# Tail copies on GpSimd, two tiles that begin with main rows, a new slot plan, and W1 cast by columns in a fused attention and mixer kernel

## The chip, the cores and the metric

The kernel runs on one core of a Trainium2 chip. The metric is the device time in microseconds of one execution; a figure for a kernel is the median of several runs. The engines are TensorE (PE, matmuls and transposes), VectorE (DVE), ScalarE (ACT), GpSimd (POOL) and SyncE (SP, which here only issues DMAs).

## The reference

S = 2048 tokens, D = 576, F = 4608, fp32.

```python
xn = layernorm(x)
# A: sliding attention, 32 heads of 18, 8 keys at a distance of 2
qkv = xn @ wqkv                      # 576 x 1728
o = local_attention(q, k, v)         # each token sees itself and 7 earlier ones, 2 apart
A = o @ wo
# B: spatial shift mixer and MLP, on xn
h = gelu(layernorm(xn) @ w1)         # 576 x 576
hs = shift(h, +1, -1, +2, -2 by quarters of the columns) @ w2
x1 = xn + hs
B = x1 + gelu(layernorm(x1) @ w3) @ w4
out = x + A + B
```

## The kernel before

**Numbers.** fp32 operands are split into a high and a low part (hi is a rounded copy made by ScalarE, lo the difference made by VectorE), and each product is a handful of matmuls of such parts (`PAIRS`, `HALVES`). 576 = 4 × 128 + 64; the last rows of a contraction, the tails, are laid beside each other in one more block.

**Order.** Nothing is scheduled by a tool: every engine runs its instructions in the order in which the program names them, with waits where one engine needs another's tile. Plans (dictionaries from a unit's or slot's number to calls) say which side work is named behind which piece of TensorE's work.

**Prologue and plain units (0 to 90 us).** Y holds the sixteen 128-token tiles of x. `stats_x` and `norm_x` normalise a tile in place: VectorE makes the statistics, GpSimd the power −1/2 (L112), VectorE the product (L119). Every second `norm_x` also makes the factors `RS[1]` of the second layer norm, with VectorE's addition of 1e-5 (L220) between GpSimd's operations. `prep_x` turns a tile: `turned` first lets ScalarE copy the tails into a tile stg, four times beside each other (L286), then TensorE transposes four main blocks (L292) and two tail blocks (L294) into PSUM, and `cast_a` splits these into the operand xt. A unit `q_plain` is one token tile by one column group (288 columns) of wqkv: 14 matmuls (L363), a copy to stg and a DMA to the DRAM tensor qkvd. There are 36 units, and five stg tiles in all, which tail copies and results share.

**The p loop (90 to 208.7 us).** For the tiles 6 to 15 the product is done in Strassen-Winograd form: a pair of token tiles (p = 3 to 7) by three column groups, seven products of 7 matmuls each (`step`, L504), 21 slots for a p. PSUM has the banks ca, cb and cc, two each, and one bank pair pp, in which the next pair is turned: `low2` (the odd tile) and `up2` (the even one), each followed by sums that VectorE and ScalarE write to a region of Y (`raw_s`) and by casts to xt (`cast_upper`, `cast_s`). ScalarE and VectorE copy or add the products into keep tiles (L515, L531, L537), which SP spills to qkvd (L348).

**Turned tiles of the second norm.** `z_turn(t)` scales a tile by ScalarE (z, L467), and VectorE transposes it by 32 x 32 blocks into st (L128, L129), one buffer for four tiles. After every fourth, `put` writes st to DRAM as xd with four DMAs (L136). `get` loads xd again as the operand z of the mixer, and `split_x` casts it.

**W1 and Y.** W1 is loaded into Y[0:5] in the loop, so these tiles of Y are first copied to DRAM (`away`, ysp, L474), and loaded back after W1 is cast (`split_w1`, L495).

**The mixer (208.7 to 268 us)** goes over four blocks of 512 tokens; a block has four tiles of 14 matmuls by W1 (L638) and one of 9 by W1R, the remaining columns (L653). Its casts and loads are named between these tiles. The stages after that (W2, MLP with attention beside it) are not touched.

SP's queue is in order, and every DMA on it waits for the one issued eight before it.

Of the kernel before, what the change touches and what calls it, by code (L numbers as in the profile page):

```python
# [57 lines left out]
def fused_block(ctx, tc, x, wqkv, wo, w1, w2, w3, w4, out):  # L58
# [27 lines left out]
    mhalf = base.tile([128, 1], F32, name="mhalf")  # L86
    sgn = base.tile([128, 1], F32, name="sgn")
# [105 lines left out]
    XO = {"A11": 0, "A12": 1, "A22": 2, "S1": 4, "S2": 5, "S3": 6, "S4": 7}  # L193
    rawp = tc.tile_pool(name="rawp", bufs=1, reuse_waits="tile")
# [14 lines left out]

    def stats_x(t):  # L210
        stats(Y[:, t, :], 0, t)

    def norm_x(t):
        norm(Y[:, t, :], Y[:, t, :], 0, t)
        if t % 2:
            two = slice(t - 1, t + 1)
# [3 lines left out]
            dve.tensor_scalar(r, r, 1e-5, None, op0=ALU.add)  # L220
            for k in (t - 1, t):
                pool.tensor_tensor(RS[1][:, k, 1:2], RS[1][:, k, 0:1], mhalf, op=ALU.pow)
# [60 lines left out]
    def turned(t, ps):  # L283
        y = Y[:, t, :]
        tails = stage_tile()[:, 0:256]
        act.copy(tails.rearrange("p (k r c) -> p k r c", k=2, r=4),  # L286
                 y.rearrange("p (k c) -> p k c", k=2)[:, :, None, 256:]
                 .to_broadcast([128, 2, 4, 32]))
        for k in range(2):
            for m in range(2):  # L290
                c = k * HF + 128 * m
                pe.transpose(ps[:, k, 128 * (m + 1):128 * (m + 2)], y[:, c:c + 128], ident)  # L292
        for k in range(2):
            pe.transpose(ps[:, k, 0:128], tails[:, 128 * k:128 * (k + 1)], ident)  # L294
# [11 lines left out]

    def prep_x(t):
        ps = psb.tile([128, 2, 512], F32, name="ps", tag="b")
        turned(t, ps)
        xo, o = plain_x(t)  # L310
        cast_a(xo, o, 2, ps)
# [43 lines left out]
    def q_plain(t, cg, mid=None):  # L355
        ps = psa.tile([128, 512], F32, name="p1", tag="a")
        xo, o = plain_x(t)
        W, w = WB[cg % 3], OP["B12"] if cg > 2 else OP["B11"]
        for i, (k, a, v) in enumerate(PLAIN):
            if mid and i == 7:  # L360
                mid()
            n = 128 if a else 96
            pe.matmul(ps[:, :QB], xo[:n, o + k, a, :], W[:n, w + k, v, :],  # L363
                      start=i == 0, stop=i == len(PLAIN) - 1)
        stg = stage_tile()
        act.copy(stg, ps[:, :QB])
        spill(stg, t, cg * QB, QB)

# [26 lines left out]
    norm_x(0)  # L395
    norm_x(1)
    for k in range(2):
        hi_main(qraw[0], 0, OP["B11"], k)
        lo_main(qraw[0], 0, OP["B11"], k)
    prep_x(0)  # L400
    split_tail(qraw[0], 0, OP["B11"])
    stats_x(2)
    prep_x(1)
    load_cg(1, raw_rows(10))
    sp.dma_start(dram_ap(qkvd[8:9, 0:1, :], 0, [[(HALO + S) * GC, 16], [1, HALO * GC]]), zpad)
# [9 lines left out]
    def upper(p):  # L415
# [3 lines left out]
    mids = {1: lambda: prep_x(2), 2: lambda: prep_x(3), 19: lambda: prep_x(4),  # L419
            20: lambda: prep_x(5), 28: lambda: lower(3), 30: lambda: upper(3)}  # L420
    plan = {0: ((norm_x, 2), (stats_x, 3), (load_cg, 4, raw_rows(13))),
            1: ((norm_x, 3), (load_x, 4)),
# [5 lines left out]
            9: ((stats_x, 4),), 10: ((split_cg, 4),), 11: ((norm_x, 4), (load_x, 6)),  # L428
            12: ((sums_b, 1, 0),), 13: ((sums_b, 1, 1),),
            14: ((split_cg, 2),), 15: ((split_t, 1, False), (load_x, 7)),  # L430
            16: ((stats_x, 5),), 17: ((norm_x, 5), (load_x, 8)), 18: ((split_cg, 5),),
            20: ((sums_b, 2, 0), (load_x, 9)), 21: ((sums_b, 2, 1),), 22: ((stats_x, 6),),
            23: ((stats_x, 7),), 24: ((norm_x, 7),), 25: ((norm_x, 6),),
            26: ((split_t, 0, True),), 27: ((split_t, 2, False),), 29: ((split_t, 1, True),),
            30: ((lambda: cast_upper(3, two[3]),),), 31: ((cast_s, 3, 0),),
            32: ((cast_s, 3, 1),), 33: ((cast_s, 3, 2),), 34: ((split_t, 2, True),),
            35: ((stats_x, 9), (stats_x, 8))}
    for n, (t, cg) in enumerate(units):
        q_plain(t, cg, mids.get(n))
        for f, *args in plan.get(n, ()):  # L440
            f(*args)
# [5 lines left out]
    room(q2pool)  # L447
    psq = tc.tile_pool(name="psq", bufs=1, space=PSUM, reuse_waits="tile")
# [14 lines left out]
    ysp = [dram.tile([128, D], F32, name=f"ysp{t}") for t in range(5)]  # L463

    def z_turn(t):
        z = q2pool.tile([128, D], F32, name="z", bufs=2)
        act.activation(z, Y[:, t, :], AF.Identity, scale=RS[1][:, t, 1:2])  # L467
        turn(z, t % 4)
        if t % 4 == 3:
            put(("z", t // 4))  # L470
# [17 lines left out]
    def split_w1(k):  # L488
        src = Y[:, k, :].rearrange("p (g c) -> p g c", g=4)
        hi = W1[:, k, 0:512].rearrange("p (g c) -> p g c", g=4)  # L490
        lo = W1[:, 5 + k, 0:512].rearrange("p (g c) -> p g c", g=4)
        split_w(hi, lo, src[:, :, :128])
        rem = W1R[:, k, :].rearrange("p (g c) -> p g c", g=4)
        split_w(rem[:, :, 0:16], rem[:, :, 16:32], src[:, :, 128:144])
        sp.dma_start(Y[:, k, :], ysp[k])  # L495
# [67 lines left out]
    for p in range(3, 8):  # L563
        n = p + 1
        plan = {}
        if n < 8:
            plan = {0: ((norm_x, 2 * n + 1),), 1: ((norm_x, 2 * n),), 5: ((low2, n),),
                    9: ((up2, n),), 10: ((lambda n=n: cast_upper(n, two[n]),),),
                    12: ((cast_s, n, 0),), 13: ((cast_s, n, 1),), 14: ((cast_s, n, 2),)}
            for k, t in zip((7, 11, 15, 17), range(4 * (p - 3), 4 * (p - 3) + 4)):  # L570
                plan[k] = plan.get(k, ()) + ((z_turn, t),)
            if n < 7:
                plan[2] = ((load_x, 2 * n + 3), (load_x, 2 * n + 2))
                plan[18] = ((stats_x, 2 * n + 3),)
                plan[19] = ((stats_x, 2 * n + 2),)
            if p == 3:
                plan[16] = ((away, 0, 3),)
            if p == 4:
                plan[12] += ((away, 3, 5),)
            if p == 6:  # L580
                plan[15] += ((load_w1,),)
        else:
            plan = {5: ((lambda: get(("z", 0), ring_block(("z", 0))),),),
                    12: ((open_w1,), (split_w1, 0)), 13: ((split_w1, 1),),
                    14: ((lambda: split_x(xring["z", 0], 0),),),
                    15: ((split_w1, 2),), 16: ((lambda: split_x(xring["z", 0], 1),),),
                    17: ((split_w1, 3),), 18: ((split_w1, 4),)}
# [1053 lines left out]
```

## Time and profile before

| | |
|---|---|
| runs | 1294.77 us median of 3 (1292.19 to 1296.27) |
| profiled execution, own time | 1291.73 us |
| its span | 1290.0 us |
| mean granted TensorE clock | 0.997 |
| TensorE busy | 1257.8 us, 98% |
| VectorE, ScalarE, GpSimd busy | 72%, 60%, 20% |
| TensorE idle 0 to 20, 20 to 90, 90 to 208.7, 208.7 to 268 us | 6.2, 3.7, 10.2, 0 us |

The table's last row is the length of a stretch less TensorE's busy time in it. In the views that follow, L504 is line 504 of the program, `ca<-wb,xt` names output and inputs, x7 is a count of instructions. A row of waits gives who waited for whom, the total in us, how often, and the longest. A row of the timeline gives start, length, engine, line and operation, and in brackets the idle time ahead of it with its releaser. SPq is the issue of DMAs by SP; a DMA's landing is told apart from its issue.

### The profile page before, as it was taken

The page shows a single profiled execution, that of the slowest core. Times are in us where ns is not written, and L with a number is a line of the kernel's source. Part 1 is how long each engine was busy: PE and PEld are TensorE (multiplying, and loading weights), DVE is VectorE, ACT ScalarE, POOL GpSimd, SP SyncE. Part 2 cuts the span into 40 slices and gives each one's busy share as a digit, 9 for nine tenths or more (in the row PEclk, how much of TensorE's full clock was granted, in tenths as well). Part 3 has the DMA queues.
Part 4 walks back from the last instruction along what each step waited for, and adds up shares of the span by engine and source line. Part 5 has one row for each costly group of instructions (what it writes and reads, how often), then busy time and mean ns, then how long its engine had stood idle before and what let it go on. Part 6 is the DMA issues. An engine that isn't in the chain of part 4 may idle for free.

```text
span 1290.0 us, 21004 instructions
## 1 busy us (share of the span) xinstructions
PE 1257.8 (98%) x7819; PEld 1155.1 (90%) x7819; DVE 933.3 (72%) x1219; ACT 773.2 (60%) x1297; POOL 255.2 (20%) x382
## 2 busy tenths in 40 slices
PE   8999998999999999999999999999999999999998
PEld 7988897899898989999889999998888999998898
DVE  6866644677638998999558998988898884465341
ACT  4455546643654655454867777777767777677730
POOL 2011100012031221121222332231223222222200
PEclk9999999999999999999999999999999999999999
DMA  8536688426788879679759889878948868899982
GB/s 228 138 83 152 160 191 212 128 65 191 213 221 206 194 134 208 119 154 211 171 100 231 170 177 240 188 139 207 283 79 186 161 113 179 187 211 218 258 253 83
DMA packets 207789, 227.14 MB, mean 176 GB/s; under 512 B 80824, under 2 KB 142232, under 8 KB 207560
## 3 DMA queue, kind: packets, MB, share of 16 engines
q1 hardware_dynamic: 174936, 159.02, 43.0%
q0 software_dynamic: 32752, 66.80, 32.3%
q8 instruction: 61, 1.00, 0.3%
q14 instruction: 40, 0.33, 0.1%
HBM read 126.83 MB, written 109.35 MB: 183 GB/s over the span
## 4 chain that ended last, share of the span: by engine, by line
PE 59%; DMA 5%; ACT 2%; DVE 2%; issue 1%; SPq 1%; DVEq 0%; ACTq 0%; POOLq 0%
PE ps L1039 28%; PE cc L1301 17%; PE p L1003 9%; PE ps L182 4%; DMA w3st<-in_B_w_dram 2%; DMA Y<-od 1%; SPq L1349 1%; DMA xt<-xn 1%; DMA xd<-big 0%; DVE w3st L1136 0%; DMA xt<-td0T 0%; DMA x1n<-td1T 0%; DVE xt L768 0%; ACT Y L1044 0%; PE p L1608 0%
## 5 line engine op out<-in xcount | busy, mean ns | idle before, releaser
L1039 PEld LDWEIGHTS ps<-w,c 128*128 128x128 f32 x3456 | 476.0, 188 | 23.2 <-ACT ev L1044 2.0
L1039 PE MATMUL ps<-w,c 128*128 128x288 f32 x3456 | 487.4, 295 | 6.6 <-ACT ev L1044 1.8
L1045 POOL DMA_DIRECT2D yd<-Y x154 | 138.1, 900 | 395.1 <-ACT Y L1044 320.1
L997 DVE TENSOR_TENSOR c<-Y,c 128x512 fp32r<-128x512 f32 x144 | 98.8, 687 | 88.5 <-ACT Y L986 87.2
L1044 ACT COPY Y<-ps 128x576 f32<-128x576 f32 x154 | 98.0, 637 | 75.7 <-PE ps L1039 63.2
L1301 PE MATMUL cc<-xt,w3s 128*128 128x512 f32 (+1 forms) x504 | 128.0, 394 | 1.0 <-DVE Y L1311 1.0
L1301 PEld LDWEIGHTS cc<-xt,w3s 128*128 128x128 f32 (+1 forms) x504 | 92.2, 188 | 19.4 <-DVE Y L1311 1.4
L1047 ACT COPY Y<-ps 128x576 f32<-128x576 f32 x92 | 59.0, 641 | 66.2 <-PE ps L1039 64.8
L1301 PE MATMUL cc<-x1n,w3a 128*128 128x512 f32 (+1 forms) x336 | 86.5, 396 | 0.5 <-ACT cc L1504 0.4
L917 DVE TENSOR_TENSOR po<-q,k 128x1152 f32<-128x1152 f32 (+1 forms) x48 | 84.2, 1755 | 0.8
L920 DVE TENSOR_REDUCE L<-po 128x64 f32<-128x1152 f32 (+1 forms) x48 | 84.0, 1751 | 0.8
L985 ACT ACTIVATE c<-p 128x512 fp32r<-128x512 f32 x48 | 28.7, 598 | 84.3 <-PE p L1003 84.3
L1311 DVE TENSOR_TENSOR Y<-cc,Y 128x512 f32<-128x512 f32 x49 | 33.7, 688 | 59.0 <-ACT Y L1307 54.8
L893 DVE TENSOR_TENSOR po<-v,L 128x1152 f32<-128x1152 f32 x56 | 75.4, 1354 | 0.9
L1301 PEld LDWEIGHTS cc<-x1n,w3a 128*128 128x128 f32 (+1 forms) x336 | 61.0, 190 | 11.8 <-ACT cc L1504 0.6
L363 PE MATMUL p<-wb,xt 128*128 128x288 f32 (+1 forms) x504 | 71.0, 301 | 0.0
L504 PE MATMUL ca<-wb,xt 128*128 128x288 f32 x420 | 63.9, 300 | 7.1 <-DVE keep L515 5.2
L363 PEld LDWEIGHTS p<-wb,xt 128*128 128x128 f32 (+1 forms) x504 | 69.0, 192 | 0.6 <-DVE wb L250 0.4
L897 DVE TENSOR_TENSOR po<-po 128x1152 f32<-128x1152 f32 x49 | 66.4, 1355 | 0.9
L504 PEld LDWEIGHTS ca<-wb,xt 128*128 128x128 f32 x420 | 57.4, 188 | 10.3 <-DVE keep L515 8.2
L112 POOL TENSOR_TENSOR rs<-rs,mhalf 128x1 f32<-128x1 f32 x32 | 19.4, 606 | 238.0 <-DVE rs L111 131.4
L1020 ACT COPY ps<-Y 128x576 f32<-128x576 f32 x92 | 59.4, 645 | 4.4 <-DVE Y L1050 2.4
(247 smaller groups left out, 2141.7 us busy)
## 6 DMA issues: line engine op xcount, KB each, us to landing
yd<-Y POOLq DMA_DIRECT2D x156, 288.0 KB, 6.1
Y<-in_B_w_dram SPq DMA_DIRECT2D x29, 576.0 KB, 5.7
w3st<-in_B_w_dram SPq DMA_DIRECT2D x56, 256.0 KB, 8.2
qkvd<-stg SPq DMA_DIRECT2D x66, 144.0 KB, 2.9
yd<-ev POOLq DMA_DIRECT2D x26, 288.0 KB, 6.9
w3st<-in_B_w_dram SPq DMA_DIRECT2D x92, 64.0 KB, 7.8
xd<-st SPq DMA_DIRECT2D x16, 320.0 KB, 5.6
xd<-big SPq DMA_DIRECT2D x16, 320.0 KB, 6.5
```

Of the source, the lines that this page charges most:

```text
L363: pe.matmul(ps[:, :QB], xo[:n, o + k, a, :], W[:n, w + k, v, :], start=i == 0, stop=i == len(PLAIN) - 1)
L504: pe.matmul(ps[:, :QB], xo[:n, XO[x], a, :], W[:n, OP[w], v, :], start=start and i == 0, stop=stop and i == len(HALVES) - 1, skip_group_ch ...
L893: dve.tensor_tensor(dst, vv, Lf[:, :, w:w + 1].to_broadcast([128, TPP * GH, HD]), op=ALU.mult)
L897: dve.tensor_tensor(o, o, dst, op=ALU.add)
L917: dve.tensor_tensor(dst, qf[:, None, :].to_broadcast([128, n, TPP * GC]), win, op=ALU.mult)
L920: dve.tensor_reduce(Lw[:, w:w + n, :], dst.rearrange("p w (x d) -> p w x d", d=HD), axis=AX.X, op=ALU.add)
L997: dve.tensor_tensor(h[:, 1, :], g, h[:, 0, :].bitcast(F32), op=ALU.subtract)
L1003: pe.matmul(ps, W3[f][:, w, :], x1n[b][:, a, :], start=n == 0, stop=n == len(PAIRS) - 1)
L1039: pe.matmul(ps[:, k, :HF], h[:, col], w[:, p, k * HF:(k + 1) * HF], start=n == 0 and not seed, stop=n == len(seq) - 1, skip_group_check=True)
L1044: act.copy(e.rearrange("p (h c) -> p h c", h=2), ps[:, :, :HF])
L1045: pool.dma_start(yd[t], e, accum_op=ALU.add)
L1301: pe.matmul(ps, WX[w][:k, v, SLOT[w], :], area[sb][xk][:k, a, :], start=onto is None and i == 0, stop=last and i == len(HALVES) - 1, skip_ ...
```

## The change

The tail copies go from ScalarE to GpSimd and are named some slots ahead of the transposes (`tails`); in the p loop they have a tile of their own, tl. GpSimd also adds the 1e-5 of the second norm. The prologue turns the main rows of tiles 0 and 1 first and does twelve of fourteen matmuls of two units before the tails are transposed; several loads change their places. In the plain units statistics and norms come a tile sooner. In the p loop all slots are set anew, `put` is called from the plan, `away` copies eight tiles rather than five and stands behind the put, and W1 is loaded a stage sooner and cast by blocks of columns, three of the five parts in the mixer's first block. All eight tiles come back in one call, `back`.

```diff
-        dve.tensor_scalar(r, r, 1e-5, None, op0=ALU.add)    # norm_x, second norm
+        pool.tensor_tensor(r, r, eps, op=ALU.add)
...
-        tails = stage_tile()[:, 0:256]                       # turned
-        act.copy(tails..., y[..., 256:] 4 times)
+    def tails(t):
+        r = tl[t] = stage_tile()[:, 0:256] if q2pool is None else q2pool.tile(
+            [128, 256], F32, name="tl")
+        pool.tensor_copy(r..., Y[:, t, 256:] 4 times)
...
-        t = 13 if p < 5 else 0                               # raw_s
+        t = {3: 13, 4: 13, 5: 0, 6: 5, 7: 5}[p]
...
-    prep_x(0)
-    split_tail(qraw[0], 0, OP["B11"])
-    stats_x(2)
-    prep_x(1)
+    turn_x(0)
+    turn_x(1)
...
+    q_part(pq[0], 0, 0, 0, 12)
+    turn_tail(0, turns[0])
+    turn_tail(1, turns[1])
...
+    q_part(pq[1], 1, 0, 0, 12)
+    norm_x(2)
+    tails(2)
+    q_part(pq[0], 0, 0, 12, 14)
+    q_leave(pq[0], 0, 0)
+    q_part(pq[1], 1, 0, 12, 14)
+    stats_x(3)
+    turn_x(2)
+    turn_tail(2, turns[2])
+    q_leave(pq[1], 1, 0)
+    norm_x(3)
+    tails(3)
...
-    def split_w1(k):                                         # one of 5 row blocks, then its tile of Y back
-        ...
-        sp.dma_start(Y[:, k, :], ysp[k])
+    def split_w1(m):
+        if m < 4:
+            c = slice(128 * m, 128 * m + 128)
+            split_w(W1[:, 0:5, c], W1[:, 5:10, c], Y[:, 0:5, 144 * m:144 * m + 128])
+        else:                                                # the remaining columns, W1R
+    def back():
+        for t in range(8):
+            sp.dma_start(Y[:, t, :], ysp[t])
...
-            plan = {0: ((norm_x, 2 * n + 1),), 1: ((norm_x, 2 * n),), 5: ((low2, n),),
-                    9: ((up2, n),), 10: ((lambda n=n: cast_upper(n, two[n]),),),
-                    12: ((cast_s, n, 0),), 13: ((cast_s, n, 1),), 14: ((cast_s, n, 2),)}
-            for k, t in zip((7, 11, 15, 17), range(4 * (p - 3), 4 * (p - 3) + 4)):
-                plan[k] = plan.get(k, ()) + ((z_turn, t),)
+            plan = {k: ((z_turn, t),) for k, t in zip((1, 9, 10, 17), zs)}
+            plan.update({0: ((norm_x, 2 * n),), 3: ((low2, n),), 4: ((tails, 2 * n),),
+                         7: ((up2, n),), 8: ((lambda n=n: cast_upper(n, two[n]),),),
+                         14: ((cast_s, n, 0),), 15: ((cast_s, n, 1), (cast_s, n, 2))})
+            plan[17] += ((put, ("z", p - 3)),)
             if n < 7:
-                plan[2] = ((load_x, 2 * n + 3), (load_x, 2 * n + 2))
-                plan[18] = ((stats_x, 2 * n + 3),)
-                plan[19] = ((stats_x, 2 * n + 2),)
-            if p == 3:
-                plan[16] = ((away, 0, 3),)
+                plan[4] += ((stats_x, 2 * n + 3),)
+                plan[16] = ((stats_x, 2 * n + 2),)
+                plan[17] += ((norm_x, 2 * n + 3), (tails, 2 * n + 3))
+            plan[18] = {3: ((load_x, 13), (load_x, 12), (away, 0, 3)),
+                        4: ((load_x, 15), (load_x, 14), (away, 3, 5))}.get(p, ())
...
-            if p == 6:
-                plan[15] += ((load_w1,),)
+            if p == 5:
+                plan[11] = ((load_w1,),)
...
+            if b == 0 and i < 3:                             # mixer, behind tile i of block b
+                split_w1((2, 4, 3)[i])
+            if (b, i) == (0, 3):
+                back()
```

**VectorE, from the last z_turn of p3 to the first of p4.** `st<-z` is the transposed tile, `keep<-cc` and `keep<-ca` the additions of slots of the product, `Y<-pp` and `xt<-pp` the work on the odd tile that low2 turned, L110 to L112 or L109 to L111 statistics. In brackets stands which counters an instruction waits for; DMAHW are DMAs. Before, from the start of p4's low2:

```order
154 L515 TENSOR_TENSOR keep<-cc_1342,keep 128x288 [waits DMAHW6_49,PE_49]
155 L322 TENSOR_TENSOR Y<-pp,Y 128x384 [waits DMAHW4_49,Activation_49]
156 L299 TENSOR_TENSOR xt<-pp,xt 128x256 [waits Activation_49]
157 L301 TENSOR_TENSOR xt<-pp,xt 32x128
158 L515 TENSOR_TENSOR keep<-ca_1425,keep 128x288 [waits DMAHW0_49,PE_49]
159 L128 STREAM_TRANSPOSE st<-z 128x16x32 [waits DMAHW2_49,DMAHW1_49,DMAHW7_49,DMAHW0_49,Activation_49]
160 L129 STREAM_TRANSPOSE st<-z 128x4x32
161 L328 TENSOR_TENSOR Y<-Y,pp 128x384 [waits DMAHW5_49,DVE_49,PE_49]
```

And now, from the last z_turn of p3 on:

```order
142 L129 STREAM_TRANSPOSE st<-z 128x16x32 [waits Activation_49]
143 L130 STREAM_TRANSPOSE st<-z 128x4x32
144 L120 TENSOR_SCALAR Y<-Y,mv_77,rs_80 128x576 [waits Pool_49]
145 L592 TENSOR_TENSOR keep<-cc_1169,keep 128x288 [waits PE_49]
146 L592 TENSOR_TENSOR keep<-ca_1340,keep 128x288 [waits PE_49]
147 L120 TENSOR_SCALAR Y<-Y,mv_77,rs_80 128x576 [waits Pool_49]
148 L129 STREAM_TRANSPOSE st<-z 128x16x32 [waits DMAHW6_49,DMAHW5_49,DMAHW7_49,DMAHW4_49,Activation_49]
149 L130 STREAM_TRANSPOSE st<-z 128x4x32
150 L358 TENSOR_TENSOR Y<-pp,Y 128x384 [waits DMAHW3_49,Activation_49]
151 L326 TENSOR_TENSOR xt<-pp,xt 128x256 [waits PE_49,Activation_49]
152 L328 TENSOR_TENSOR xt<-pp,xt 32x128
153 L592 TENSOR_TENSOR keep<-cc_1352,keep 128x288
```

The transpose that writes st again, which waits for the four DMAs of the put, stood behind low2's operations and stands ahead of them now.

**SP, around the first put, at the end of p3.** `xd<-st` is the put, `qkvd` the spills, `ysp` the copies of Y, `in_A_x` the loads of x. Before:

```order
40 L474 DMA ysp_1164<-Y 128x576
41 L474 DMA ysp_1165<-Y 128x576
42 L474 DMA ysp_1166<-Y 128x576
43 L136 DMA xd<-st 32x20x128 x4
44 L348 DMA qkvd<-keep 128x4x72
```

And now:

```order
40 L137 DMA xd<-st 32x20x128 x4
41 L384 DMA qkvd<-keep 128x4x72
42 L210 DMA Y<-in_A_x_dram 128x576 x2
43 L547 DMA ysp_1171<-Y 128x576
44 L547 DMA ysp_1172<-Y 128x576
45 L547 DMA ysp_1173<-Y 128x576
46 L384 DMA qkvd<-stg 128x4x72
```

The three copies of Y stood ahead of the put and stand behind it now, with a spill and two loads of x between.

**SP in the mixer's first block.** `v<-u` are moves for the remaining columns, `xt<-xd` the loads of the operand z of the block after the next. Before:

```order
122 L659 DMA v<-u 16x512
123 L141 DMA xt<-xd 128x3x512
124 L141 DMA xt<-xd 128x2x512
125 L624 DMA w2r<-in_B_w_dram 128x576 x2
126 L658 DMA v<-u 16x512
```

And now:

```order
119 L736 DMA v<-u 16x512
120 L572 DMA Y<-ysp_1171 128x576
121 L572 DMA Y<-ysp_1172 128x576
122 L572 DMA Y<-ysp_1173 128x576
123 L572 DMA Y<-ysp_1174 128x576
124 L572 DMA Y<-ysp_1175 128x576
125 L572 DMA Y<-ysp_1176 128x576
126 L572 DMA Y<-ysp_1177 128x576
127 L572 DMA Y<-ysp_1178 128x576
128 L142 DMA xt<-xd 128x3x512
129 L142 DMA xt<-xd 128x2x512
130 L701 DMA w2r<-in_B_w_dram 128x576 x2
```

The eight loads of Y stand ahead of the operand's loads; before, five such loads stood among the last spills of the p loop.

More of the change, by code (lines that the diff above doesn't have):

```diff
@@ L208, in load_x @@
         sp.dma_start(Y[:, t, :], xf[t * 128:(t + 1) * 128, :])
+    counted, scaled = set(), {}
     def stats_x(t):
         stats(Y[:, t, :], 0, t)
+        counted.add(t)
     def norm_x(t):
         norm(Y[:, t, :], Y[:, t, :], 0, t)
-        if t % 2:
-            two = slice(t - 1, t + 1)
+        lo = t - t % 2
+        if not scaled.get(lo) and counted >= {lo, lo + 1}:
+            scaled[lo] = True
+            two = slice(lo, lo + 2)
             r = RS[1][:, two, 0:1]
@@ L367, in q_plain @@
         spill(stg, t, cg * QB, QB)
+    def q_plain(t, cg, mid=None):
+        ps = psa.tile([128, 512], F32, name="p1", tag="a")
+        q_part(ps, t, cg, 0, 7)
+        if mid:
+            mid()
+        q_part(ps, t, cg, 7, 14)
+        q_leave(ps, t, cg)
     load_x(0)
@@ L395, in fused_block @@
     norm_x(0)
+    tails(0)
     norm_x(1)
-    for k in range(2):
-        hi_main(qraw[0], 0, OP["B11"], k)
-        lo_main(qraw[0], 0, OP["B11"], k)
-    prep_x(0)
-    split_tail(qraw[0], 0, OP["B11"])
-    stats_x(2)
-    prep_x(1)
+    tails(1)
+    r0 = qraw[0]
+    hi_main(r0, 0, 0, 0)
+    lo_main(r0, 0, 0, 0)
+    turn_x(0)
+    turn_x(1)
+    act.copy(flat(plain_x(0)[0][:, 0:2, 3:5, :]), turns[0][:, :, 128:384])
+    hi_main(r0, 0, 0, 1)
+    lo_main(r0, 0, 0, 1)
+    dve.tensor_tensor(flat(plain_x(0)[0][:, 0:2, 1:3, :]), turns[0][:, :, 128:384],
+                      flat(plain_x(0)[0][:, 0:2, 3:5, :]).bitcast(F32), op=ALU.subtract)
+    cast_x(1)
+    pq = [psa.tile([128, 512], F32, name="p1", tag="a") for t in range(2)]
+    q_part(pq[0], 0, 0, 0, 12)
+    turn_tail(0, turns[0])
+    turn_tail(1, turns[1])
+    split_tail(r0, 0, 0)
+    cast_x(0, True)
+    stats_x(2)
+    cast_x(1, True)
+    q_part(pq[1], 1, 0, 0, 12)
[10 more added lines that the diff above has]
+    tails(3)
+    xo, o = plain_x(2)
+    cast_a(xo, o, 2, turns[2])
     load_cg(1, raw_rows(10))
+    load_cg(4, raw_rows(13))
+    load_x(4)
     sp.dma_start(dram_ap(qkvd[8:9, 0:1, :], 0, [[(HALO + S) * GC, 16], [1, HALO * GC]]), zpad)
@@ L462, in fused_block @@
     W1 = W1R = w1p = None
-    ysp = [dram.tile([128, D], F32, name=f"ysp{t}") for t in range(5)]
+    ysp = [dram.tile([128, D], F32, name=f"ysp{t}") for t in range(8)]
     def z_turn(t):
```

103 lines of the change are left out of this document (59 added, 44 removed).

## The prediction, made before the changed kernel was run

> **What bounds the kernel now.** I read the page first, then the busy time by stages, then TensorE's waits, then the timeline around the places that the change touches. The page says that TensorE is the bound:
>
> ```profile
> PE 1257.8 (98%) x7819; PEld 1155.1 (90%) x7819; DVE 933.3 (72%) x1219; ACT 773.2 (60%) x1297; POOL 255.2 (20%) x382
> ```
>
> By stages (columns: length, then busy time of PE, PEld, DVE, ACT, POOL, the granted clock, DMA share, GB/s):
>
> ```profile
> 20.00:90.00 70.00, 66.28 (x493) 65.00 (x492) 51.28 (x82) 37.92 (x84) 6.32 (x13) 1.00 0.50 123
> 90.00:208.70 118.70, 108.47 (x786) 103.32 (x785) 70.84 (x165) 63.16 (x149) 12.46 (x26) 1.00 0.75 178
> 208.70:268.00 59.30, 59.30 (x263) 48.90 (x262) 35.41 (x49) 34.91 (x58) 0.67 (x16) 1.00 0.43 124
> ```
>
> The change edits only the first 268 us. There TensorE idles 3.7 us in the plain units (20 to 90), 10.2 in the p loop (90 to 208.7) and nothing in the mixer. All that can be won is therefore small and sits in named waits (total us, times, longest), 0 to 270 us:
>
> ```profile
> PE ps L294 <- ACT stg L286: 6.5, 5, 1.4
> PE ca L504 <- DVE keep L515: 5.2, 13, 1.1
> PE pp L294 <- ACT stg L286: 2.5, 7, 0.4
> PE ca L504 <- ACT keep L537: 1.9, 1, 1.9
> PE ps L292 <- DVE rs L220: 0.9, 1, 0.9
> PE pp L292 <- DVE Y L119: 0.7, 1, 0.7
> ```
>
> Two rows are the tail copies that ScalarE makes just before TensorE transposes them; two are additions into the keep tiles that VectorE reaches late. Asked by stretch, the first row has 3.7 us in the plain units (20 to 90), so 2.8 in the prologue, and the second 1.7 in the last stage (p7, from 178):
>
> ```profile
> PE ps L294 <- ACT stg L286: 3.7, 3, 1.3
> PE ca L504 <- DVE keep L515: 1.7, 3, 1.1
> ```
>
> **The p3/p4 boundary of before**, from the timeline; the argument rests on it:
>
> ```profile
> 111.23 4.63 SPq L136 DMA_DIRECT2D xd<-st  x4
> 112.72 1.09 PE L504 MATMUL cc<-wb,xt 128*128 128x288 f32 x7
> 114.28 2.12 PE L504 MATMUL ca<-wb,xt 128*128 128x288 f32 x14 [0.47 <-DVE keep L515]
> 115.95 1.62 SPq L348 DMA_DIRECT2D qkvd<-keep  x1
> 116.24 1.10 PE L504 MATMUL cc<-wb,xt 128*128 128x288 f32 x7
> 117.18 1.09 PE L504 MATMUL cb<-wb,xt 128*128 128x288 f32 x7
> 117.67 1.88 SPq L348 DMA_DIRECT2D qkvd<-stg  x1
> 119.53 0.48 ACT L321 COPY Y<-pp 128x384 f32<-128x384 f32 x1 [0.53 <-PE pp L294]
> 120.04 0.56 DVE L322 TENSOR_TENSOR Y<-pp,Y 128x384 f32<-128x384 f32 x1 [2.21 <-ACT Y L321]
> 120.64 0.37 ACT L297 CAST xt<-pp 128x256 fp32r<-128x256 f32 x1 [0.62 <-DVE Y L322]
> 120.90 0.27 ACT L298 CAST xt<-pp 96x128 fp32r<-96x128 f32 x1
> 121.20 0.42 DVE L299 TENSOR_TENSOR xt<-pp,xt 128x256 fp32r<-128x256 f32 x1 [0.60 <-ACT xt L298]
> 121.64 0.29 DVE L301 TENSOR_TENSOR xt<-pp,xt 32x128 fp32r<-32x128 f32 x1
> 122.55 0.71 DVE L128 STREAM_TRANSPOSE st<-z 128x512 f32<-128x512 f32 x1
> ```
>
> A slot is 7 matmuls, 0.94 us from start to start (116.24 to 117.18). The slot at 112.72 took 1.56 us for a wait of 0.47, so a wait costs 0.15 us beside its length. The cb at 117.18 is slot 5 of p4. Nine slots of 0.94 and that loss of 0.62 lie between it and TensorE's start of slot 17 of p3, which was therefore at 108.1. Call that T. The put of the turned tile st, behind the fourth z_turn in slot 17, starts at T+3.1. Its last two DMAs, the later issued at 114.3 (the second and third line of a question on this line and stretch):
>
> ```profile
> L136 SPq DMA_DIRECT2D xd<-st x2: 1507/1664/1822, 112.5 to 114.3; - x2
> DMA to landing us min/median/max: 6.4/6.4/6.4
> ```
>
> So the put has landed at 114.3 + 6.4 = 120.7, T+12.6. The next write into st starts at 122.55, behind that. st has one buffer, so the kernel of before only just keeps clear of this wait.
>
> **The change part by part.**
>
> *Tails on GpSimd.* In the plain units the three waits for stg (3.7, with 3 × 0.15 of restart 4.15) go, but the casts around unit 28 stay late by my reading of VectorE's queue there (about 0.65 kept): −3.5. In the p loop the seven waits of 2.5 go too. GpSimd's price for a 128x256 copy is not in the trace; the nearest rows:
>
> ```profile
> L222 POOL TENSOR_TENSOR rs<-rs,mhalf 128x1 f32<-128x1 f32 x10 | 6.9, 705 | 2.9 <-DVE rs L220 2.9
> L388 POOL MEMSET Y<- 16x1008 f32 x1 | 0.9, 928 | 0.1
> masks.py:199 POOL TENSOR_SCALAR_AFFINE_SELECT ident<-ident 128x128 f32<-128x128 f32 x1 | 0.3, 292 | 0.1
> L286 ACT COPY stg<-Y 128x256 f32<-128x256 f32 x8 | 3.3, 408 | 0.2 <-DVE Y L119 0.2
> ```
>
> I bound it by 0.3 and 0.9 and take 0.5, nearest to the two rows with 128 partitions. GpSimd is 20% busy and the copies are issued one to several slots ahead, so this is covered; without the cover it is 0.5 for each of 14.
>
> [...]
>
> *Prologue.* Main rows of tiles 0 and 1 first, twelve matmuls ahead of the tails. TensorE loses 2.8 to stg, 0.9 to rs. VectorE's chain (stats, norm of four tiles, W1's first lo parts) is not shortened much; behind it GpSimd's queue becomes late: tails(3) stands behind four pow (0.705 each) and three small operations. Value −0.9, bounds 0 and −2.5.
>
> *p loop, old waits.* Slots move: low2 to 3, up2 to 7, the casts behind the additions. Of 10.2 us, 3.6 lie in p7 and 6.6 in p3 to p6, in 18 waits, so 9.3 with restarts. I give all back but about 1.2 at the up2 of p3, where VectorE still works off split_t(2,True), statistics and norm: −8.1. In p7 the additions of the last two groups stay late: −1.5.
>
> *p loop, new wait.* The first z_turn of p4, p5, p6 goes from slot 7 to slot 1, four slots behind the put instead of ten. VectorE's transpose into st waits for all four DMAs of the put; in VectorE's queue behind it stand low2's addition, its lo casts, an addition into keep, statistics. pp has one buffer, so up2's transposes (slot 7) wait for these. Slot 1 ends at T+5.6, ScalarE's z comes behind it, and VectorE is at the transpose at about T+7; it stands until the landing at T+12.6 to 13.2 (norm(2n+3) and a spill now lie near the put), say 12.9. From there 0.71, 0.3 for the transpose's small half (an estimate: a quarter of the elements and a start), 0.56, 0.64 for ScalarE's casts, 0.42 and 0.29 make 2.9: pp is free at T+15.8. TensorE reaches up2 after the twelve slots 17 to 20 and 0 to 7 (11.3) and low2's six transposes (at most 0.9, since seven matmuls of 288 columns take 0.94): T+12.2. The stall is 3.6, with the restart and the late addition into keep 4.0. Bounds: 1, if the put lands two to three us sooner, and 6, at its longest.
>
> *The clock on top.* From the start of the trace (the figure before the DMA share is the granted clock):
>
> ```profile
> 7.58:10.99 3.41, 0.88 (x7) 0.65 (x7) 2.48 (x6) 2.71 (x6) 1.81 (x3) 1.00 1.11 305
> 10.99:14.40 3.41, 3.41 (x15) 3.41 (x16) 3.24 (x8) 0.85 (x2) 0.55 (x1) 0.50 1.01 307
> ```
>
> A stretch of 3.41 us in which TensorE was 26% busy was followed by one at half clock, which costs up to 1.7 us of matmuls. A stall of 4 us leaves some such stretch at under 40%. I add 1.1 for each of three (0 to 1.7). [...]
>
> *ysp.* low2 of p4 writes its raw sums into Y[0:3], which away(0,3) must have copied to ysp before. In before these three stood ahead of the put; now they stand behind it, a spill and two x loads on SP's queue. Issues behind the put took 1.62 and 1.88 (quoted), since each waits until an earlier one has landed. Sizes and landing:
>
> ```profile
> ysp<-Y SPq DMA_DIRECT2D x5, 288.0 KB, 4.0
> xd<-st SPq DMA_DIRECT2D x16, 320.0 KB, 5.6
> ```
>
> Put issued by T+7.9, spill T+9.5, two x T+11.5, two ysp T+14, landed T+18 (17 to 20). ScalarE's copy needs the second one: 0.48 + 0.56 + 0.64 + 0.71 and hand-overs: pp free T+20.7. At p4 the stall is thus 8.6 instead of 4.0.
>
> *W1 by columns, ysp back.* In the mixer's first block the rest of W1 is cast between tiles, ScalarE and VectorE behind split_x(z1). The remainder tile waits: +2.1, the last +0.5, bounds 0 and 4. Then all eight reloads of Y stand on SP ahead of the loads of z2:
>
> ```profile
> 227.00 1.07 SPq L141 DMA_DIRECT2D xt<-xd  x2
> DMA to landing us min/median/max: 4.7/4.7/4.7
> Y<-ysp SPq DMA_DIRECT2D x5, 288.0 KB, 3.6
> ```
>
> The DMA rate in forty slices of 190 to 270 us:
>
> ```profile
> GB/s 199 240 176 347 333 244 326 235 200 233 210 75 323 407 175 0 29 53 49 196 398 209 0 8 179 53 61 200 405 171 18 8 53 53 33 57 56 13 0 0
> ```
>
> Eight times 288 KB are 2.36 MB; at the 300 to 400 GB/s of the busiest slices that is 6 to 8 us, and z2 lands at about 240 instead of 231.7 (227.0 + 4.7). ScalarE stands in split_x(z2), gelu behind it, and TensorE runs out at the third block's first tile. That tile begins ten tiles of about 3.2 us (14 matmuls of 0.23) behind 208.7, near 240.5, and needs its casts of z2 some 3 to 4 us behind the landing: +3.5, bounds 0 and 7.
>
> **Sum.** Gains 0.9 + 3.5 + 8.1 + 1.5 = 14.0. New: p4 8.6 + 1.1, p5 and p6 2 × 5.1, mixer 2.6, z2 3.5, together 26.0. Net +12.0 on the profiled execution's own 1291.73 us: 1303.7. That execution lies 3.0 under the median of the runs shown (1294.77); on the median it is 1306.8. I forecast 1305.
>
> **The rivals.**
> 1. *Faster: VectorE never stands long at st.* If the put lands at T+9 or earlier (its DMAs no longer share the engines with ysp, which stood ahead of it), only gains and the mixer count: −14.0 + 2.6 + 0.4 = −11, about 1282. It decides at a landing near T+9.3, where pp comes free (2.9 later) as TensorE arrives. For it: three ysp copies are gone from ahead of p3's put. Against: the sixteen put DMAs of all four stages have a median landing of 5.6 (quoted), at p3 6.4, and only p3 had ysp ahead; four of 320 KB took 4.6 us to issue alone. 0.18.
> 2. *No change: the new waits are there but half as long* (put landing at T+11, no clock penalty, ysp hidden by it): new 3 × 2 + 2.6 + 3.5 + ysp 2 = 14, net 0: 1292 to 1296. 0.10.
> 3. *Heavier queue:* SP's lanes slip, ysp lands at T+20, z2 comes 7 late, clock falls each time: +24, about 1317. 0.10.
> 4. [...] 0.04.
> 5. The change does not do what it says: the instruction order shows the moves, so I give this nothing of its own.
>
> **How the numbers follow.** The likeliest case (0.58) has 1296 to 1314 as its own range from the bounds of the stalls. The range that holds 8 in 10 leaves out the core of rival 1 and the tail of rival 3: 1287 to 1317. 0.3% is 3.9 us, about what can be told from no change. Faster 0.19, same 0.11, slower 0.70.
>
> **What would show it.** Right: VectorE's first st<-z of p4 to p6 idle for about 6 us with the put as releaser; PE waits on pp of about 4, 4 and, at p4, 8 us; no waits for stg or tl; ACT waiting at z2's load near 240. Wrong: TensorE's waits in 90 to 208 us sum to under 8 us, or the st transposes start without idle time.

## The result and the profile after

The changed kernel takes 1308.65 us (median of 4 runs, 1308.12 to 1310.07), the kernel before 1294.3: a ratio of 1.0113 [1.0095, 1.0131], or 14.4 us more. Forecast were 1305 and a range of 1287 to 1317. The profiled execution's span is 1307.1 us at a mean granted clock of 0.987.

Busy time by stage, first the changed kernel, then the kernel before, each cut where TensorE starts the p loop, the mixer and the stage after it (length, busy PE, PEld, DVE, ACT, POOL, granted clock, DMA share, GB/s):

```profile
0.00:85.80 85.80, 79.83 (x577) 76.86 (x578) 64.50 (x113) 42.70 (x92) 20.29 (x62) 1.00 0.64 164
85.80:215.80 130.00, 112.47 (x786) 110.60 (x785) 67.62 (x149) 57.23 (x132) 14.64 (x37) 0.91 0.68 157
215.80:283.80 68.00, 63.32 (x262) 50.37 (x261) 37.22 (x51) 36.55 (x61) 0.62 (x16) 0.95 0.44 136
283.80:1303.90 1020.10, 1012.94 (x6201) 928.15 (x6199) 763.43 (x894) 629.66 (x993) 228.80 (x292) 1.00 0.79 181
```

```profile
0.00:90.10 90.10, 80.17 (x576) 77.97 (x577) 63.83 (x113) 45.90 (x100) 14.78 (x48) 0.98 0.58 150
90.10:208.70 118.60, 108.37 (x785) 103.22 (x784) 70.75 (x165) 63.06 (x148) 12.46 (x26) 1.00 0.75 178
208.70:267.90 59.20, 59.20 (x263) 48.80 (x262) 35.31 (x48) 34.91 (x58) 0.67 (x16) 1.00 0.43 124
267.90:1286.40 1018.50, 1010.04 (x6201) 925.10 (x6199) 762.94 (x895) 629.34 (x993) 227.28 (x292) 1.00 0.80 182
```

Prologue and plain units gain 4.3 us, the p loop loses 11.4, the mixer 8.8, and the untouched rest 1.6. In the p loop TensorE idles 17.5 instead of 10.2 us, and the clock, 1.00 before, is 0.91. The main rows of TensorE's waits in the first 270 us of the changed kernel, to be held against those of before:

```profile
PE pp L303 <- DVE xt L328: 14.7, 3, 7.6
PE ps L715 <- ACT g L721: 2.9, 1, 2.9
PE ps L730 <- DVE W1R L169: 1.7, 1, 1.7
PE ps L303 <- DVE Y L120: 1.5, 3, 0.8
PE ca L581 <- DVE keep L592: 1.3, 2, 0.8
PE ps L307 <- POOL stg L295: 1.0, 1, 1.0
PE pp L307 <- POOL tl L295: 1.0, 1, 1.0
```

Most of the small waits for the tail copies and for keep are gone: of 9.0 us for the copies 2.0 are left (1.0 for stg in the prologue and 1.0 for tl early in the p loop), of VectorE's 5.2 for keep 1.3. Three waits of up2 for pp stand in their place. The timeline shows what VectorE (DVE), ScalarE and SP did meanwhile, at p4 and, in the last two lines, at p5:

```profile
106.33 4.13 SPq L137 DMA_DIRECT2D xd<-st  x4
112.35 2.40 SPq L210 DMA_DIRECT2D Y<-in_A_x_dram  x2
114.80 1.42 SPq L547 DMA_DIRECT2D ysp<-Y  x3
115.79 0.71 DVE L129 STREAM_TRANSPOSE st<-z 128x512 f32<-128x512 f32 x1 [7.81 <-DMA xd<-st]
119.63 0.48 ACT L357 COPY Y<-pp 128x384 f32<-128x384 f32 x1 [8.94 <-DMA ysp<-Y]
122.23 1.09 PE L303 MATMUL pp<-ident,Y 128*128 128x128 f32 x4 [7.58 <-DVE xt L328]
...
146.36 0.71 DVE L129 STREAM_TRANSPOSE st<-z 128x512 f32<-128x512 f32 x1 [7.34 <-DMA xd<-st]
149.24 1.09 PE L303 MATMUL pp<-ident,Y 128*128 128x128 f32 x4 [3.56 <-DVE xt L328]
```

VectorE stands 7.8 us at the first transpose into st until the put has landed, ScalarE 8.9 us until ysp has, and TensorE 7.6 and 3.6 us until VectorE has emptied pp. In p4's stall the clock falls (four stretches of 3.41 us; the clock stands ahead of the DMA share):

```profile
113.75:117.16 3.41, 0.90 (x7) 0.65 (x5) 0.91 (x2) 0.00 (x0) 0.00 (x0) 1.00 0.90 233
117.16:120.57 3.41, 0.00 (x0) 0.00 (x0) 0.43 (x1) 0.48 (x1) 0.00 (x0) 0.50 1.11 359
120.57:123.99 3.42, 1.76 (x8) 1.79 (x9) 2.65 (x9) 1.13 (x4) 0.18 (x1) 0.50 0.36 68
123.99:127.40 3.41, 3.41 (x16) 3.41 (x16) 2.26 (x6) 1.41 (x4) 0.37 (x1) 0.50 0.40 99
```

A stretch with 26% of TensorE work is followed by three at half clock. The last of them is full of work that goes at half speed: 1.7 us lost. By TensorE's start-to-start times the matmuls in half-clock stretches lost 2.4 us at p4, 2.5 at p5, 2.6 at p6 and 3.0 in the mixer. The mixer's own stall, on ScalarE and TensorE:

```profile
247.14 0.62 ACT L149 CAST xt<-xt 64x512 fp32r<-64x512 f32 x1 [5.90 <-DMA xt<-xd]
...
250.94 9.29 PE L715 MATMUL ps<-xt,W 128*128 128x512 f32 x27 [2.90 <-ACT g L721]
```

### The profile page after: what moved, and what is told of

It is laid out like the page before. It is cut to its first block, busy times and chain, and to the rows that moved or that the text cites. A ratio compares the mean times of both kernels' runs of the same rounds, so it can differ in the third digit from the quotient of the medians.

```text
span 1307.1 us, 21009 instructions
## 1 busy us (share of the span) xinstructions
PE 1268.6 (97%) x7819; PEld 1166.0 (89%) x7819; DVE 933.2 (71%) x1206; ACT 766.1 (59%) x1276; POOL 264.3 (20%) x407
## 4 chain that ended last, share of the span: by engine, by line
PE 63%; issue 3%; ACT 2%; DVE 2%; DMA 1%; POOL 0%; DVEq 0%; POOLq 0%; ACTq 0%
PE ps L1120 30%; PE cc L1382 19%; PE p L1084 10%; PE ps L183 4%; DMA yd<-Y 1%; DVE xt L849 0%; DVE w3st L1217 0%; POOL yd L1126 0%; ACT Y L1125 0%; PE p L1689 0%; ACT xt L1179 0%; ACT Y L1067 0%; DVE c L1078 0%; DVE Y L1131 0%; ACT c L1072 0%
## 5 line engine op out<-in xcount | busy, mean ns | idle before, releaser
L581 PEld LDWEIGHTS ca<-wb,xt 128*128 128x128 f32 x420 | 61.2, 200 | 2.7 <-DVE keep L592 1.8
```

Source lines behind the costliest of these rows:

```text
L581: pe.matmul(ps[:, :QB], xo[:n, XO[x], a, :], W[:n, OP[w], v, :], start=start and i == 0, stop=stop and i == len(HALVES) - 1, skip_group_ch ...
```

## The experiments

The theory: the loss is time in which VectorE and ScalarE, in order, stand at an instruction that waits for DMAs of SP's queue (the put, ysp, z2), and the half clock behind each stall. The rivals: slower puts whoever waits, or too much casting in the mixer.

Differences are taken from the changed kernel's 1308.65 us. The kernel before took 1294.3 us beside it, but 1293.85 beside runs 1 to 4, 1293.01 beside 5 to 8 and 1292.97 beside 9 to 11, so up to 1.3 us of such a difference need not come from the edit. Runs 8, 9 and the comparisons with the kernel before go by the time beside them.

**1. z_turn's slots undone.**

```diff
-plan = {k: ((z_turn, t),) for k, t in zip((1, 9, 10, 17), zs)}
+# z_turn in slots 7, 11, 15, 17, as in the kernel before
```

> The changed kernel with z_turn named in slots 7, 11, 15 and 17 again, as in the kernel before; all else as changed. Theory (TensorE's stalls come from VectorE standing at the transpose into st until the put has landed): the stalls of 3.7 us at p5 and p6 go, with the half-clock matmuls behind them (2.5 us each), so 12.5 us less than 1308.65: about 1296. The stall at p4 stays at 7 to 8 us, since ScalarE's copy there waits for ysp and not for the put. Rival A (the puts themselves or the spills run slower than before, whoever waits): the stalls only move to another tile and the time stays at 1306 to 1310. [...]

1305.03 us (1304.04 to 1307.44), 3.6 less where 12.5 were expected. TensorE's waits in 95 to 190 us:

```profile
PE pp L303 <- DVE xt L328: 7.3, 1, 7.3
PE ca L581 <- DVE keep L592: 3.2, 1, 3.2
PE cc L581 <- DVE keep L592: 1.6, 3, 0.6
```

The stall at p6 is gone and that at p4 stays, as expected. But at p5 one of 3.2 us is left under another name. VectorE's timeline there:

```profile
149.81 0.82 DVE L110 BATCH_NORM_STATS2 bn<-Y 128x6 f32<-128x288 f32 x2 [3.82 <-DMA Y<-in_A_x_dram]
150.67 0.21 DVE L111 BATCH_NORM_AGGREGATE mv<-bn 128x2 f32<-128x12 f32 x1
150.91 0.16 DVE L112 TENSOR_SCALAR rs<-mv 128x1 f32<-128x1 f32 x1
150.99 0.46 DVE L592 TENSOR_TENSOR keep<-ca,keep 128x288 f32<-128x288 f32 x1
```

The statistics of the odd tile, now in slot 4, wait for its load, which stands behind the put on SP. It stood behind the put in the kernel before too (slot 2 of the next p), but the statistics came only in slot 18. I had not seen this wait: it lay hidden behind that for st. The theory in its first form, one cause for p5 and p6, falls. p6 has no such load, and there nothing is left. The p loop takes 124.9 us, 5.1 less than the changed kernel's; behind p5's stall matmuls still run at half speed (six of 128x288 took 1.81 us from 151.50 us, where seven take 1.09 at full clock in the kernel before), and the clock over the p loop is 0.95.

**2. The ysp copies ahead of the put.**

```diff
+            if p == 3:
+                plan[16] = ((away, 0, 3),) + plan.get(16, ())
-            plan[18] = {3: ((load_x, 13), (load_x, 12), (away, 0, 3)),
+            plan[18] = {3: ((load_x, 13), (load_x, 12)),
```

> The changed kernel with the three copies of Y[0:3] to ysp named ahead of the put again (slot 16 of p3); all else as changed. Theory: the stall at p4 falls from 7.7 us to that of p5 and p6, 3.7 us, perhaps 4.5 since the put now starts behind three more DMAs; p5, p6 and the mixer stay. 3 to 4.5 us less than 1308.65: 1304 to 1306. Rival (the put alone makes all of the stall at p4, ysp is hidden in it): unchanged, 1308 to 1310. Rival B (the place of ysp decides all three stalls through SP's queue): 15 us less.

1304.76 us (1304.42 to 1309.1), 3.9 less, as expected. The three waits for pp fall from 14.7 to 12.4, p4's from 7.6 to 5.0, somewhat more than the 3.7 to 4.5 expected to be left:

```profile
PE pp L303 <- DVE xt L328: 12.4, 3, 5.0
```

**3. Useless matmuls in the stall, first try.** They stand in the queue right ahead of up2's transposes and go to unused columns of the open bank ca, whose product they also disturb.

```diff
     def up2(p):
...
+        for _ in range(FILL[p - 5]):           # 62, 27, 27
+            pe.matmul(wide[g][:, QB:512], ...)
```

> The changed kernel with matmuls of no use ahead of up2's transposes, in TensorE's own queue and into columns of a bank that nothing reads: 62 of 224 columns at p4 and 27 each at p5 and p6, about 6.2 and 2.7 us of work, a little less than the stalls there. The output does not change. Theory (a stall costs its length and, behind it, 2.5 us of matmuls at half clock, because TensorE was busy for 26 to 36% of the 3.4 us before): the clock stays at 1.00 in 90 to 208 us, the stalls' ends stay where they are, and 7 to 7.5 us go: 1301 to 1302. Rival (the slow matmuls come from something else at these places, such as the DMA traffic): the time stays at 1308 to 1310. If the useless matmuls outlast the stalls or their operands are late, up to 3 us are given back.

1323.05 us, 14.4 more. The matmuls wrote to a bank that ScalarE had still to copy (cb<-ca), so they waited for it until the stall was over (3.3 us at p5) and then ran at about half speed, 27 of them for 5.8 us (3.2 us in run 7, at a clock of 1.00). A miss of the design; it says nothing on the clock.

**4. The reloads of Y behind the loads of z2.**

```diff
-            if (b, i) == (0, 3):
-                back()
...
                 get(("z", b + 2), ring_block(("z", b + 2)))
+                if b == 0:
+                    back()
```

> The changed kernel with the eight reloads of Y behind the loads of z2 in SP's queue, not ahead of them; all else as changed. Theory: z2 lands some 7 us sooner, the wait of 2.9 us at the first tile of the mixer's third block goes with the half-clock matmuls behind it (3.0): 6 us less, about 1302.5. The wait for W1R (1.7) stays. Rival (ScalarE's and VectorE's additional casts of W1 make the third block late, not z2's landing): 0 to 1 us less, 1307 to 1309.

1303.25 us (1301.8 to 1303.88), 5.4 less. In the mixer the stall for z2 is gone and that for W1R is left:

```profile
PE ps L730 <- DVE W1R L169: 2.0, 1, 2.0
PE ps L730 <- DVE xt L156: 0.2, 1, 0.2
```

The mixer takes 63.3 us instead of 68.0, which is 4.7 of the 5.3 us by which the profiled execution is shorter; with the wait for W1R left, the clock over the mixer is 0.97 (0.95 in the changed kernel). The p loop is the changed kernel's own, and yet the clock behaves differently in it. p5's stall, 3.5 us long as before, falls across the border of two stretches:

```profile
145.02:148.44 3.42, 1.70 (x13) 1.46 (x11) 1.05 (x3) 0.00 (x0) 0.00 (x0) 1.00 0.97 206
148.44:151.85 3.41, 1.59 (x13) 1.57 (x13) 2.64 (x9) 1.13 (x4) 0.01 (x1) 1.00 1.06 338
```

They have 50 and 47% of TensorE work, and the clock stays at 1.00. In the changed kernel the same stall left one stretch with 36% (1.22 us from 144.46 us on), and two at half clock followed (147.88 to 154.70 us).

**5. z_turn's slots undone, and SP's order at p3 and p4.**

```diff
+# z_turn in slots 7, 11, 15, 17
-            plan[18] = {3: ((load_x, 13), (load_x, 12), (away, 0, 3)),
-                        4: ((load_x, 15), (load_x, 14), (away, 3, 5))}.get(p, ())
+            plan[16] = plan.get(16, ()) + {the same}.get(p, ())     # ahead of the put
```

> The changed kernel with z_turn in slots 7, 11, 15, 17 as in the kernel before, and with the loads of x and the copies to ysp of p3 and p4 named in slot 16, ahead of the put; all else as changed. Theory, mended after the first runs (three waits on DMAs of SP's queue lie one behind the other at these places: st for the put, the raw sums for ysp, the statistics of the odd tile for its load; whichever is taken away alone, the next holds VectorE): the stalls of 7.7, 3.7 and 3.7 us go together with 7.5 us of half-clock matmuls, less about 1.5 for additions that are late: 21 us less than 1308.65, about 1287. Rival (the put lands late whatever stands ahead of it, and everything on VectorE behind slot 17 waits): at most 9 us less, 1300 or more.

1291.28 us (1289.3 to 1293.57): 17.4 less, where runs 1 and 2 saved 3.6 and 3.9 alone. The p loop falls from 130.0 to 110.2 us, more than 8 below the kernel before; up2 no longer waits for pp, and 1.0 us for tl is left. The run moves more than runs 1 and 2 together: the loads of x and p4's copies to ysp go ahead of the put as well, and no run has the first two alone. The mixer takes 68.2 us, as long as the changed kernel's 68.0: its stall for z2 is longer (3.3 and a wait of 1.2 for casts), but the clock stays at 1.00.

```profile
86.40:196.60 110.20, 105.38 (x785) 103.36 (x784) 66.99 (x149) 57.44 (x132) 14.64 (x37) 1.00 0.81 185
196.60:264.80 68.20, 60.72 (x263) 48.37 (x262) 37.26 (x52) 36.50 (x61) 0.62 (x16) 1.00 0.43 135
```

**6. All three undone.** Runs 5 and 4 together.

> The same, and the eight reloads of Y behind the loads of z2. Theory: the sum of both, 21 and 5.4 us less than the changed kernel, 1281 to 1283, and 11 to 13 less than the kernel before: what the change gains in the prologue, the plain units and the p loop without its new waits. Rival (the gains are bound to the new waits, since VectorE and ScalarE only shift their work): 1290 or more.

1283.83 us (1282.89 to 1285.2), against the kernel before 0.9928 [0.9913, 0.9943], 9.2 less where 11 to 13 were expected: most of what the change gains is there once these waits are gone. That for W1R (2.0 us) is still in it, and additions into keep come late for cc (1.6 us).

**7. Useless matmuls, second try,** ahead of the first product of the slot before up2.

```diff
+            if g in FILL:                      # {13: 62, 16: 27, 19: 27}
+                for _ in range(FILL[g]):
+                    pe.matmul(ca[:, QB:512], ...)
             seven(g, ca, "A11", "B11", True, False)
```

> The changed kernel with useless matmuls again, now ahead of the first product of the slot before up2, where no engine's copy stands between: 62 at p4 and 27 each at p5 and p6, by the run before 0.108 us each at full clock, so 6.7 and 2.9 us in stalls of 7.6 and 3.6. The output does not change. Theory (too little work in the 3.4 us before sets the half clock): clock 1.00 in 90 to 210 us, the stalls shrink to about 1 us but end where they ended, 7 to 7.5 us less than 1308.65: 1301 to 1302. Rival (the clock falls at these places for another reason): 1308 to 1310.

1305.94 us (1303.72 to 1309.28), 2.7 less than the changed kernel rather than 7. The clock did what the theory says. Its p loop and the first of the fills:

```profile
85.90:211.10 125.20, 119.07 (x902) 116.52 (x901) 67.01 (x149) 56.92 (x132) 14.64 (x37) 1.00 0.71 163
```

```profile
113.65 7.08 PE L605 MATMUL ca<-wb,xt 128*128 128x224 f32 x62
122.31 0.63 PE L303 MATMUL pp<-ident,Y 128*128 128x128 f32 x4 [0.64 <-DVE xt L328]
```

With TensorE kept busy the clock is 1.00 throughout and the p loop takes 125.2 us instead of 130.0. It is 4.8 and not 7.5 because the fills (13.4 us by their rows) and what is left of the stalls outlast the old stalls. So the half clock in this p loop (0.91 in the changed kernel) is an effect of the stalls. The profiled execution is 5.2 us shorter in all (span 1301.9 against 1307.1, clock 0.996 against 0.987). It is the fastest of the four, which scatter by 5.6 us; why the median gains only 2.7 no trace shows.

**8. Tail copies alone, on the kernel before.** GpSimd makes all of them.

```diff
-        act.copy(tails..., y[..., 256:] 4 times)
+        if t not in tl:
+            tails(t)                           # GpSimd; tiles 4 to 15 named in the plans, ahead
```

> The kernel before with one part of the change alone: the tail copies by GpSimd, named ahead of the transposes (tiles 4 to 7 and all of the p loop), in the p loop into a tile of their own. Theory: the waits of 3.7 us in the plain units and of 2.5 in the p loop go, with 0.15 us of restart for each of ten, less 0.65 that stays: 7 us less than the kernel before, about 1287. [...] Rival B (the copies only uncover the next wait at the same place): 1291 to 1293.

1297.31 us (1293.28 to 1300.99), 1.0024 [1.0009, 1.0039]: a little slower, where 7 us less were expected. The profiled execution is the fastest of the ten (1293.28). TensorE's waits in the first 110 us:

```profile
PE ps L303 <- POOL stg L289: 8.9, 4, 4.7
PE pp L303 <- POOL tl L289: 2.3, 1, 2.3
```

In the old prologue the copies stand behind powers on GpSimd that wait for VectorE's statistics of the next tile:

```profile
14.73 0.55 POOL L112 TENSOR_TENSOR rs<-rs,mhalf 128x1 f32<-128x1 f32 x1 [4.70 <-DVE rs L111]
15.23 0.40 POOL L289 COPY stg<-Y 128x256 f32<-128x256 f32 x1
```

The expectation did not name this: GpSimd stood 4.7 us at the power, and the copy behind it began at 15.23 us.

**9. Tail copies alone, second try:** GpSimd copies tiles 4 to 15 only, right behind the norm (in the p loop the even tile's copy stands in slot 6).

```diff
         norm(Y[:, t, :], Y[:, t, :], 0, t)
+        if 4 <= t < 8 or t > 8 and t % 2:
+            tails(t)                           # tiles 0 to 3 keep act.copy
```

> The kernel before with the tail copies of the tiles 4 to 15 alone by GpSimd, named right behind the tile's norm and ahead of the factors of the second norm in GpSimd's queue; the prologue's four tiles keep ScalarE's copies. Theory (the gain is there, and the run before lost it in the prologue where the copies stood behind GpSimd's powers): the waits of 3.7 us in the plain units and of 2.5 in the p loop go, with ten restarts of 0.15, less 0.65: 7 us less than the kernel before, 1286 to 1287. Rival (the additions into keep come late at the same places, so that the waits only change their name): 1291 to 1294.

1286.98 us (1285.6 to 1289.21), 0.9954 [0.9939, 0.9968]: 6.0 less, as expected within 1 us. Up to the p loop it takes 85.9 us, the same as the changed kernel with its whole new prologue; the p loop 115.7.

```profile
0.00:85.90 85.90, 79.47 (x577) 77.49 (x578) 63.88 (x114) 44.28 (x96) 16.83 (x52) 1.00 0.61 157
85.90:201.60 115.70, 108.41 (x785) 104.56 (x784) 70.71 (x165) 60.40 (x140) 15.38 (x34) 0.99 0.78 185
```

**10. All three undone, tails by ScalarE.**

```diff
-        pool.tensor_copy(r.rearrange(...), ...)
+        act.copy(r.rearrange(...), ...)
```

> The kernel with all three undone (z_turn's slots, SP's order at p3 and p4, the reloads of Y) with the tail copies by ScalarE at the new places, not by GpSimd. Both engines take 0.40 us for one. Theory (what counts is that they stand ahead of the transposes; the engine does not matter, except in the prologue, where GpSimd's copy of tile 3 came 1.2 us late): 1282 to 1285, and the wait for tile 3's copy in the prologue is shorter. Rival (GpSimd takes work from a loaded ScalarE, whose copies into keep and stg then come later by 0.4 us each for 14 tiles): 1286 to 1289. [...]

1289.0 us (1286.45 to 1290.13), 5.2 more than run 6. It is the time that the rival gave, but not for its reason, since the p loop did not grow. The stages say where: 89.5 us up to the p loop (86.1 in run 6), 109.6 in the p loop (110.2), 61.8 in the mixer (62.6), 1024.2 behind it (1019.7). TensorE's largest wait in the prologue is

```profile
PE p L396 <- ACT xt L324: 2.5, 1, 2.5
```

and ScalarE's timeline ahead of it:

```profile
15.60 0.41 ACT L295 COPY stg<-Y 128x256 f32<-128x256 f32 x1 [2.74 <-DVE Y L120]
15.91 0.69 ACT L401 COPY stg<-p 128x288 f32<-128x288 f32 x2
18.06 0.40 ACT L295 COPY stg<-Y 128x256 f32<-128x256 f32 x1 [1.45 <-DVE Y L120]
18.37 0.58 ACT L324 CAST xt<-ps 128x512 fp32r<-128x512 f32 x1
```

The copies of tiles 2 and 3, named ahead, make ScalarE wait for VectorE's norms, and the results and casts queued behind them come late. So the engine does not matter in the p loop, and it does in the prologue. The 4.5 us in the untouched rest I can't ascribe to the edit: by their sizes two waits there (2.2 and 1.4, where run 6 has one of 1.5) and the lower clock (0.996 over the profiled execution and 0.999 in run 6, with 0.98 up to the p loop in both) are enough, but why they were there stays open.

**11. The remaining columns of W1 cast in p7.**

```diff
-split_w1((2, 4, 3)[i]) behind the mixer's first three tiles
+split_w1(4) in slot 18 of p7, split_w1((2, 3)[i]) behind the first two
```

> The kernel with all three undone, and the part of W1 for the remaining columns cast in p7 (slot 18), not behind the second tile of the mixer's first block; of W1's other columns the third part behind the first tile, the last behind the second. Theory: the wait for W1R (1.7 us, 2.15 from start to start) goes and p7 has room for 0.3 us of casts on each engine: 1281 to 1282. Rival (the casts delay the additions that end p7): no change, 1283 to 1285.

1282.65 us (1281.59 to 1283.56), 0.9916 [0.9903, 0.993]. The wait for W1R is gone and the mixer takes 60.1 us (run 6: 62.6), but the p loop 111.1 (110.2). Its times overlap with run 6's; both are faster than either kernel, by 9 to 10 us than the one before as timed beside them.

## Why the prediction was right, point by point

- **The new wait at st.** Right in place and size. Forecast were VectorE idle about 6 us and a stall of 4.0 at p5 and p6; measured 7.3 us and 3.6 (3.7 from start to start). Runs 1 and 5 show the cause, with one thing missed: at p5 the statistics, moved ahead by 14 slots, wait for a load of x behind the put as well, so the st wait alone is not the stall there. Of the signs that I named one failed: waits of 1.0 us each for stg and for tl are left.
- **ysp.** Forecast 8.6 at p4, measured 7.75 from start to start; ScalarE's 8.9 us at ysp are in the trace. Its copy starts 13.3 us behind the put's first issue, where I had 14.9. Run 2 takes 2.6 us of the stall away. My reason for the long issues behind the put, that each waits for an earlier landing, does not hold for the row that I quoted: the spill issued at 115.95 took 1.62 us, although the DMA eight before it had landed at 110.8. Why such issues are long stays open.
- **The clock, the term that was mis-sized.** I gave 1.1 us for each of three stalls and none for z2's. It was 2.4, 2.5, 2.6 and 3.0: 10.5 instead of 3.3. I had reckoned one half-clock stretch for a stall, and there were two, at p4 three. Run 7 shows that the stalls make it. But the price is no constant, so that the clock fell behind all four stalls is in part chance: run 4's stall at p5, as long, had no half clock, nor had z2's of 3.3 us in run 5, whose mixer has a clock of 1.00. In the changed kernel the half-clock stretches behind the four stalls begin at 117.16, 147.88, 175.18 and 250.28 us, multiples of 3.413 us apart (9, 8 and 22).
- **W1 and z2.** Forecast 2.6 and 3.5; measured 2.6 us of excess between 215.8 and 245 us, and 3.1 at z2. Run 4 shows that the reloads make the second, run 11 the cast the first.
- **Gains.** Prologue and plain units 4.4 forecast, 4.3 measured; run 9 has 85.9 us with the old prologue, so the new prologue itself is not shown to gain anything. In the p loop I gave back 9.6 of the old waits; with the stalls taken away, run 5's p loop stands 8.4 below the kernel before.
- **The sum** on the profiled execution was +12.0 and came out as +17.1 in span (+14.4 by the medians). The clock makes 7.2 of the difference and the untouched rest 1.6, less about 3.7 by which stalls were shorter and gains larger. That 1305 came so near is partly luck, since these errors stand against each other, and the profiled execution of the kernel before lay 2.6 us below its median. The 1.6 include a wait of 1.1 us at 350 us, which I did not foresee; the kernel before has one of 1.8 between 300 and 400 us, of which 0.3 is left, so where the 1.6 come from stays open.
- **The rivals.** That the put lands in time was wrong: it landed 9.0 to 9.5 us behind its first issue, and 9.5 in the kernel before. Of the heavier queue only the clock came true: ysp landed sooner, and z2 31.3 us behind the mixer's start, as I had it (240 less 208.7). With the tail copies on ScalarE instead of GpSimd (run 10) the p loop was 0.6 us shorter, too little to tell a cause. At one place of the changed kernel's trace a copy by GpSimd ran beside subtractions by VectorE:

```profile
39.31 1.10 POOL L295 COPY stg<-Y 128x256 f32<-128x256 f32 x1 [4.21 <-DVE Y L120]
39.10 3.31 DVE L279 TENSOR_TENSOR Y<-Y 128x864 f32<-128x864 f32 x3
```

The copy took 1.10 us; the other fifteen took 0.39 to 0.56. No wait of TensorE came of it.

## What to carry to other kernels

Before a step is moved, list every DMA that its first instruction waits for, on each engine, and when that lands; an engine that stands in order makes everything behind it late (at p5 VectorE stood 7.3 us at st, and TensorE 3.6 us behind it), and a DMA behind the one waited for can be a second wait hidden in the first (3.8 us for a load of x in run 1). Undoing one of several nested waits shows little: here 3.6 and 3.9 us alone, 17.4 when both were undone with the loads of x and p4's copies. A stall's price is its length and the clock behind it, and the second part is no constant: at p5 it was 2.5 us in the changed kernel, where the stall left a stretch with 36% of TensorE work, and nothing in run 4, where it left two with 50 and 47%.

## What the runs showed of the hardware

GpSimd copied 128x256 in 0.40 us (median of sixteen in the changed kernel), as fast as ScalarE (0.41, kernel before), but once, beside VectorE's subtractions at 39.10 us, in 1.10 us. A stall of 3.6 us of TensorE cost another 2.5 us of matmuls at half clock in the changed kernel (p5) and nothing in run 4 (3.5 us, clock 1.00), and at p4 the half clock lasted three stretches of 3.41 us (117.16 to 127.40 us), of which the first was spent idle itself.

In the traces of the kernel before and the changed kernel, cut into these stretches, seven at full clock had 26 to 38% of TensorE work, and half clock followed each; none had between 38 and 57%, and those with 57% (kernel before, 202.14 us) or more kept the clock. In run 4 two with 50 and 47% kept it. These few do not show a limit. A stretch at half clock with 80% of work (changed kernel, 250.28 us) was followed by another at half clock, one with 96% (kernel before, 652.70 us) by full clock.
